# Loading x two tiles per transfer, and spreading the matmuls between the one-column groups, in a fused adaLN + sliding attention + SwiGLU kernel

## Chip, cores, metric

One Trainium2 chip, one core. The metric is device time in microseconds (us).

## The reference, cut to what matters

```python
mod = (silu(c) @ w_mod).reshape(1, 6, 1, -1)       # sa, ca, ga, sb, cb, gb
h = layernorm(x) * (1 + ca) + sa                   # x: 2048 x 1024, bf16
x = x + ga * attention(h, k_cache, v_cache, wq, wo)  # 32 q heads, 4 kv heads, last 512 keys
h = layernorm(x) * (1 + cb) + sb
x = x + gb * (silu(h @ w_gate) * (h @ w_up)) @ w_down
```

Only the beginning matters here: LayerNorm of the first 512 rows of x, the scale `1 + ca` and the shift `sa` (each a matrix-vector product with w_mod), and the first eight q heads.

## The kernel before

x is loaded as 128-row tiles of 256 KB, one transfer each. The loads shown all go through one queue, in this order; SyncE issues them.

```python
xt = [xpool.tile([P, D], BF16, ...) for tt in range(S // P)]
def load_x(tt):
    fetch(out=xt[tt], in_=x2d[tt * P:(tt + 1) * P, :])

for tt in range(QT):                 # QT = 4 tiles, the first 512 rows
    load_x(tt)
for half in range(DH):               # DH = 2
    load_wm(1, half)                 # scale part of w_mod, 1 MB
    load_wq8(2 * half)               # wq of the first 8 heads, 512 KB
    load_wq8(2 * half + 1)
load_wm(0, 0); ...; load_wm(0, 1)    # shift part of w_mod, 1 MB each
# [cut: k, v, further wq]
```

LayerNorm of the four tiles is spread over the engines: tile 0 has its statistics on VectorE, tile 1 on ScalarE (a sum, then squares), both are normalised on GpSimd; tiles 2 and 3 are done on VectorE. For all four tiles ScalarE turns the variance into the scaling factor (`rstd_0`, lines `mv` in the profile). TensorE transposes them in the order 0, 1, 2, 3.

```python
stats_0(0)                # VectorE
act_sum(1)                # ScalarE
nc.scalar.copy(out=siluc, in_=sil_ps)
rstd_0(0)                 # ScalarE, needs the statistics of tile 0
stats_0(2)                # VectorE
act_squares(1)            # ScalarE
warm(3); xpose_0(0, norm_0(0))                  # GpSimd, then TensorE
rstd_0(1, 1.0 / D); rstd_0(2); warm(5)
stats_0(3)
xpose_0(1, norm_0(1)); xpose_0(2, ln_norm(2))
rstd_0(3); n3 = ln_norm(3)
mod_cols(1, 0, ca1, True, (0,))                 # first use of the scale part of w_mod
xpose_0(3, n3)
# [cut: the scaled copies hs, then q matmuls for heads 0 to 6 on contraction tiles 0 to 5]
```

The q matmuls start before the shift `sa` is known: its contribution is added as a bias. `sa_mm` computes columns of `sa` with one-column matmuls, `sa_out` copies them (two small VectorE instructions), `sh_mm` multiplies them with wq, again one column each. `q0(g, (6, 7))` are the two last 512-column matmuls of head g, put between these groups:

```python
q0(0, (6, 7)); q0(1, (6, 7))
sa_mm(0, (0, 1))
q0(2, (6, 7))
sa_mm(0, (2, 3))
sa_out(0)
q0(3, (6, 7))
sh_mm(0, range(5))                  # needs sa_out(0)
q0(4, (6, 7))
sh_mm(0, (5, 6))
# [cut: ln_mod]
sa_mm(1, (0,))
q0(5, (6, 7))
sa_mm(1, (1, 2, 3))
sa_out(1)
q0(H0 - 1, (6,)); q0(H0 - 1, (7,))  # H0 = 7
sh_mm(1, range(H0))                 # needs sa_out(1)
```

Of the kernel before, what the change touches and what calls it, by code (L numbers as in the profile page):

```python
# [11 lines left out]
BF16 = mybir.dt.bfloat16  # L12
# [576 lines left out]
def fast_path(ctx, tc, flag, A_x, A_k_cache, A_v_cache, A_wq, A_wo, B_x, B_w_gate, B_w_up,  # L589
# [4 lines left out]
    P = 128  # L594
    _, S, D = A_x.shape
    _, Hkv, Sk, Dh = A_k_cache.shape
    HD = A_wq.shape[1]
    H = HD // Dh
# [6 lines left out]
    QT = TCW // P  # L605
# [11 lines left out]
    x2d = A_x.flatten_outer_dims()  # L617
# [12 lines left out]
    xpool = ctx.enter_context(tc.tile_pool(name="xres", bufs=1))  # L630
# [21 lines left out]
    def big(name, shape=(P, 2, 512), dt=FP32):  # L652
        return psp.tile(list(shape), dt, name=name, tag="s", bufs=2)
# [6 lines left out]
    def pin(ins, what="steps"):  # L660
        return tc.keep_in_program_order(ins) if stage[what] else ins

    def fetch(out, in_):
        pin(nc.sync.dma_start(out=out, in_=in_), "dma")
# [19 lines left out]

    c_r = const.tile([DT, P], BF16, name="c_r")
    nc.scalar.dma_start(out=c_r, in_=c_v)
    xt = [xpool.tile([P, D], BF16, name=f"x{tt}", tag=f"x{tt}") for tt in range(S // P)]

    def load_x(tt):
        fetch(out=xt[tt], in_=x2d[tt * P:(tt + 1) * P, :])  # L690

    wm_tiles = {}

# [13 lines left out]
    H0 = 7  # L707
# [4 lines left out]
        load(t, wq_v[:, 2 * i:2 * i + 2, 0:8 * P])  # L712
        wq8.append(t)

    for tt in range(QT):
        load_x(tt)
    for half in range(DH):
        load_wm(1, half)
        load_wq8(2 * half)
# [115 lines left out]
    def at(k, f, *a):  # L835
        tasks.setdefault(k, []).append((f, a))
# [200 lines left out]
    def w0(g, dt):  # L1037
        return wq8[dt // 2][:, dt % 2, g * P:(g + 1) * P]

    def q0(g, dts, src=None):  # L1040
        for dt in dts:
            nc.tensor.matmul(q0_ps[g], lhsT=w0(g, dt),  # L1042
                             rhs=hs[dt // 4][:, dt % 4, :] if src is None else src[:, dt, :],
                             start=(dt == 0), stop=(dt == DT - 1 and g != H0 - 1))
# [4 lines left out]
    def sh_mm(half, heads):  # L1049
        for g in heads:  # L1050
            for i in range(4):
                dt = 4 * half + i
                nc.tensor.matmul(one_ps[:, 1 + half, g:g + 1], lhsT=w0(g, dt),  # L1053
                                 rhs=sa_bf[:, dt:dt + 1], start=(i == 0), stop=(i == 3))

    def sa_mm(half, tiles):
        for i in tiles:
            c = 4 * half + i
            for dt in range(DT):
                nc.tensor.matmul(one_ps[:, 0, c:c + 1],  # L1060
                                 lhsT=wm_tiles[(0, half)][:, dt, i * P:(i + 1) * P],
                                 rhs=siluc[:, dt:dt + 1], start=(dt == 0), stop=(dt == DT - 1))

    def sa_out(half):
        c = slice(4 * half, 4 * half + 4)
        nc.vector.tensor_copy(out=sa[:, c], in_=one_ps[:, 0, c])
        nc.vector.tensor_copy(out=sa_bf[:, c], in_=sa[:, c])
# [4 lines left out]
    for i in range(2):  # L1072
        t = big("q_ps")
# [10 lines left out]
    q0(0, (6, 7))  # L1084
    q0(1, (6, 7))
    sa_mm(0, (0, 1))
    q0(2, (6, 7))
    sa_mm(0, (2, 3))
    sa_out(0)
    q0(3, (6, 7))  # L1090
    sh_mm(0, range(5))
    q0(4, (6, 7))
# [1 line left out]
    for dt in range(4):  # L1094
        ln_mod(("h1", 0), dt, ca1, sa)
    sa_mm(1, (0,))
    q0(5, (6, 7))
    sa_mm(1, (1, 2, 3))
    sa_out(1)
    q0(H0 - 1, (6,))  # L1100
    q0(H0 - 1, (7,))
    sh_mm(1, range(H0))

    for i in range(2):
# [188 lines left out]
    for vec, dst, starts in ((2, gcol[0], (1, 9)), (4, cb1, (17, 25)), (3, sb, (33, 41)),  # L1293
# [8 lines left out]
        elif vec in (2, 5):  # L1302
            at(k, store_gate, vec // 5)
            at(k + 3, load_gate, vec // 5, gb_bc if vec == 5 else ga_bc)
    for tt in range(QT, S // P):
        cc, t = divmod(tt, QT)
        at(max((cc - 1) * H - 16, 0) + 2 + 2 * t, load_x, tt)
    for hg in range(H // 4):
        for i in range(2):
            for j in range(2):  # L1310
# [132 lines left out]
def kernel(tc, *args):  # L1443
    nc = tc.nc
    with tc.tile_pool(name="guard", bufs=1) as gp:
        flag = gp.tile([1, 1], I32, name="flag")
        over = fast_path(tc, flag, *args)
        with tc.If(over > 0):
            general_path(tc, *args)
# [30 lines left out]
```

## Time and profile before

| | before |
|---|---|
| time, median of 3 runs | 1272.11 us (1271.86 to 1272.19) |
| span of the profiled run | 1270.0 us |
| first q matmul starts | 11.43 us |
| first score matmul starts | 29.91 us |

From the profile page of the kernel before: the span, the busy time of each engine, and the chain of work that ended last.

```profile
span 1270.0 us, 18162 instructions
...
PE 1262.5 (99%) x7589; PEld 641.1 (50%) x7589; DVE 609.4 (48%) x1332; ACT 335.1 (26%) x440; POOL 4.2 (0%) x15
...
PE 99%; ACT 0%; DMA 0%; POOL 0%; issue 0%; DVE 0%; SPq 0%
```

TensorE (PE) is the limit nearly throughout. So the change can only act where PE still waits: in about the first 30 us. What is won or lost there should shift all the rest, and in the traces it does: in the nine later profiles that record every matmul, the shift against the kernel before is the same at 31 us and at the last matmul, to 0.01 us.

The timeline of TensorE before (start in us, duration in us, engine, line, operation, output<-inputs, shape, count; in brackets how long the engine was idle before it, and what ended that). L960 are the transposes, L785 and L1060 one-column products with w_mod, L1042 q matmuls, L1053 the bias columns, L1210 the first score matmuls.

```profile
9.08 1.07 PE L960 MATMUL h_ps<-ident,xn 128*128 128x128 bf16 x16 [0.23 <-POOL xn L989]
10.08 0.35 PE L785 MATMUL mod_ps<-siluc,wm 128*128 128x1 bf16 x8
...
11.43 4.58 PE L1042 MATMUL q_ps<-hs,wq 128*128 128x512 bf16 x20
15.85 0.94 PE L785 MATMUL mod_ps<-siluc,wm 128*128 128x1 bf16 x32
...
22.26 0.54 PE L1060 MATMUL one_ps<-siluc,wm 128*128 128x1 bf16 x16
...
23.50 0.59 PE L1042 MATMUL q_ps<-hs,wq 128*128 128x512 bf16 x2
24.09 0.64 PE L1053 MATMUL one_ps<-sa_bf,wq 128*128 128x1 bf16 x20
...
26.46 0.59 PE L1042 MATMUL q_ps<-hs,wq 128*128 128x512 bf16 x2
27.05 0.84 PE L1053 MATMUL one_ps<-sa_bf,wq 128*128 128x1 bf16 x28
...
29.91 1.03 PE L1210 MATMUL s_ps<-qT,kT 128*128 128x512 bf16 x4
```

How to read it: the durations of neighbouring matmuls overlap (the page gives a mean of 379 ns for one 512-column q matmul, while they start 0.216 us apart), so the distance between starts is what counts. Twenty-six q matmuls (from 16.65 us, not shown) fill the time up to 22.26 us, 0.216 us each; sixteen one-column matmuls, with their weight loads, fill 23.09 to 23.50 us (not shown), 25.6 ns each. Two q matmuls start at 23.50, so PE could go on at 23.93, but the bias columns start at 24.09: a gap of 0.16 us. The same gap stands between 26.46 + 0.43 = 26.89 and 27.05 us.

The timeline of VectorE before: statistics of tiles 0 and 2, then the normalisation of tiles 2 and 3 (one line for both).

```profile
3.49 1.29 DVE L845 BATCH_NORM_STATS2 st<-x 128x6 f32<-128x512 bf16 x2 [1.95 <-DMA x<-in_A_x_dram]
...
5.72 1.29 DVE L845 BATCH_NORM_STATS2 st<-x 128x6 f32<-128x512 bf16 x2 [0.69 <-DMA x<-in_A_x_dram]
...
8.64 1.29 DVE L864 TENSOR_SCALAR xn<-x,mv 128x1024 bf16<-128x1024 bf16 x2
```

The trace also records each of the 16 completions of a transfer; a wait ends with the last of them. In the kernel before, the x tiles were complete at 3.47, 4.09, 5.69 and 7.17 us, the first half of the scale part of w_mod at 10.03 us, the two halves of the shift part at 22.05 and 25.13 us.

### The profile page before, as it was taken

The numbers are of one execution on the slowest core, as the hardware profiler recorded it, in microseconds if no ns is written. First come the engines' busy times: TensorE is split into PE (matmuls) and PEld (weight loads), VectorE is DVE, ScalarE is ACT, GpSimd is POOL, SyncE is SP. The second block draws the span as 40 slices with busy tenths as digits, with TensorE's granted clock in tenths as the row PEclk, the third lists the DMA queues.
The fourth block names the chain that finished last, engine by engine and source line by source line (L and its number), as shares of the span: only waits on it lengthen the run. The fifth ranks groups of instructions, "written<-read, shape, count | busy, mean of one in ns | idle before, by whom it ended". The sixth has DMA issues, their size and how long they took to land.

```text
span 1270.0 us, 18162 instructions
## 1 busy us (share of the span) xinstructions
PE 1262.5 (99%) x7589; PEld 641.1 (50%) x7589; DVE 609.4 (48%) x1332; ACT 335.1 (26%) x440; POOL 4.2 (0%) x15
## 2 busy tenths in 40 slices
PE   9999999999999999999999999999999999999998
PEld 4555555555555555555554444444444444444444
DVE  5665658785678664677564631311222112221122
ACT  3543334343333433334341111011100111011100
POOL 1000000000000000000000000000000000000000
PEclk9999999999999999999999999999999999999999
DMA  9897657879456655454575479336633565425702
GB/s 290 209 252 180 166 141 168 173 165 219 121 136 175 150 138 153 113 154 113 121 206 143 136 227 247 95 95 212 211 114 105 169 213 181 158 91 168 246 15 71
DMA packets 306891, 204.46 MB, mean 161 GB/s; under 512 B 145649, under 2 KB 303345, under 8 KB 306802
## 3 DMA queue, kind: packets, MB, share of 16 engines
q1 hardware_dynamic: 301890, 199.03, 58.3%
q10 hardware_dynamic: 4912, 4.20, 1.0%
q8 instruction: 61, 1.00, 0.3%
q14 instruction: 28, 0.23, 0.1%
HBM read 165.94 MB, written 4.21 MB: 134 GB/s over the span
## 4 chain that ended last, share of the span: by engine, by line
PE 99%; ACT 0%; DMA 0%; POOL 0%; issue 0%; DVE 0%; SPq 0%
PE gu_ps L1356 30%; PE a_ps L1274 17%; PE q_ps L1199 16%; PE d_ps L1376 15%; PE o_ps L1242 9%; PE s_ps L1210 9%; PE q_ps L1042 1%; DMA x<-in_A_x_dram 0%; PE one_ps L1053 0%; PE mod_ps L785 0%; PE one_ps L1060 0%; PE h_ps L960 0%; ACT junk L981 0%; POOL xn L989 0%; ACT junk L975 0%
## 5 line engine op out<-in xcount | busy, mean ns | idle before, releaser
L1212 ACT ACTIVATE pT<-s_ps 128x1024 bf16<-128x1024 f32 x256 | 249.4, 1020 | 347.4 <-PE s_ps L1210 347.4
L1274 PE MATMUL a_ps<-wo,oT 128*128 128x512 bf16 x1024 | 241.9, 379 | 0.0
L1199 PE MATMUL q_ps<-hT,wq 128*128 128x512 bf16 x960 | 227.1, 379 | 0.0
L1362 DVE TENSOR_TENSOR guT<-gu_ps,sg 128x512 bf16<-128x512 f32 x112 | 77.5, 692 | 286.8 <-ACT sg L1361 286.7
L1356 PE MATMUL gu_ps<-hT,wg 128*128 128x512 bf16 x896 | 211.7, 379 | 0.0
L1361 ACT ACTIVATE sg<-gu_ps 128x512 bf16<-128x512 f32 x112 | 66.9, 597 | 488.7 <-PE gu_ps L1356 480.1
L1376 PE MATMUL d_ps<-wd,guT 128*128 128x512 bf16 (+2 forms) x952 | 194.2, 366 | 0.0
L1356 PE MATMUL gu_ps<-hT,wu 128*128 128x512 bf16 x672 | 163.3, 379 | 0.0
L1274 PEld LDWEIGHTS <-oT 128*128 128x128 bf16 x1024 | 100.2, 98 | 120.6
L946 DVE CAST qT<-q_ps 128x512 bf16<-128x512 f32 x121 | 83.6, 691 | 154.8 <-PE q_ps L1199 154.5
L1199 PEld LDWEIGHTS <-wq 128*128 128x128 bf16 x960 | 93.9, 98 | 113.3
L1376 PEld LDWEIGHTS <-guT 128*128 128x128 bf16 x952 | 90.9, 98 | 102.9
L1242 PEld LDWEIGHTS <-pT 128*128 128x128 bf16 x2048 | 126.6, 98 | 30.2
L1356 PEld LDWEIGHTS <-wg 128*128 128x128 bf16 x896 | 87.6, 98 | 105.5
L1242 PE MATMUL o_ps<-v_sb,pT 128*128 128x129 bf16 x2048 | 137.0, 220 | 0.0
L1210 PE MATMUL s_ps<-qT,kT 128*128 128x512 bf16 x512 | 131.5, 379 | 0.0
L1356 PEld LDWEIGHTS <-wu 128*128 128x128 bf16 x672 | 65.8, 98 | 79.3
L1229 DVE TENSOR_TENSOR oq<-o_ps,rl 128x256 bf16<-128x256 f32 (+2 forms) x256 | 100.6, 419 | 3.9
L1380 DVE TENSOR_TENSOR f<-d_ps,gb_bc 128x512 f32<-128x512 f32 (+2 forms) x34 | 22.4, 660 | 140.8 <-PE d_ps L1376 140.8
L1210 PEld LDWEIGHTS <-kT 128*128 128x128 bf16 x512 | 44.9, 98 | 30.9 <-issue 0.5
L1282 DVE TENSOR_TENSOR acc<-a_ps,acc 128x512 f32<-128x512 f32 x64 | 44.0, 688 | 32.6 <-PE a_ps L1274 32.6
L1356 PE MATMUL gu_ps<-hT,v_sb 128*128 128x512 bf16 x224 | 57.5, 379 | 0.0
(101 smaller groups left out, 426.7 us busy)
## 6 DMA issues: line engine op xcount, KB each, us to landing
wq<-in_A_wq_dram SPq DMA_DIRECT2D x64, 512.0 KB
wo<-in_A_wo_dram SPq DMA_DIRECT2D x64, 512.0 KB
wg<-in_B_w_gate_dram SPq DMA_DIRECT2D x56, 512.0 KB
wd<-in_B_w_down_dram SPq DMA_DIRECT2D x56, 512.0 KB
wu<-in_B_w_up_dram SPq DMA_DIRECT2D x42, 512.0 KB
v_sb<-in_B_w_up_dram SPq DMA_DIRECT2D x14, 512.0 KB
x<-in_A_x_dram SPq DMA_DIRECT2D x16, 256.0 KB
wm<-in_w_mod_dram SPq DMA_DIRECT2D x4, 1024.0 KB
```

The source lines that it names most:

```text
L946: nc.vector.tensor_copy(out=t, in_=q_ps)
L1199: nc.tensor.matmul(q_ps, lhsT=w, rhs=hT[("h1", cc)][:, dt, :], start=(dt == 0), stop=(dt == DT - 1))
L1210: nc.tensor.matmul(s_ps[:, i, :], lhsT=kT[:, kv, j * P:(j + 1) * P], rhs=qT[g], start=True, stop=True)
L1212: nc.scalar.activation(out=p[:, 2 * jj:2 * jj + 2, :], in_=s_ps, func=ACT.Exp, scale=scale)
L1229: nc.vector.tensor_tensor(out=dst, in0=ps[:, s0:s0 + cnt, 0:Dh], in1=sc, op=ALU.mult)
L1242: nc.tensor.matmul(o_slot["ps"][:, s_, :], lhsT=pT[g][:, j, t * P:(t + 1) * P], rhs=v_sb[:, kv, j, 0:VN], start=(j == 0), stop=(j == WT - 1))
L1274: nc.tensor.matmul(a_ps, lhsT=oT[(cc, 2 * q + i)][:, hh % 4, t * P:(t + 1) * P], rhs=wo_tiles[(cc, q, dh, i)][:, hh % 4, :], start=(hh == ...
L1282: nc.vector.tensor_tensor(out=acc[(cc, t)][:, dsl], in0=a_ps, in1=acc[(cc, t)][:, dsl], op=ALU.add)
L1356: nc.tensor.matmul(ps[:, n, :], lhsT=gu_w[(cc, fg, nm, dt // 4)][:, dt % 4, fi * P:(fi + 1) * P], rhs=hT[("h2", cc)][:, dt, :], start=(dt ...
L1361: nc.scalar.activation(out=g, in_=ps[:, 0, :], func=ACT.Silu)
L1362: nc.vector.tensor_tensor(out=guT[(cc, fg)][:, fi, :], in0=ps[:, 1, :], in1=g, op=ALU.mult)
L1376: nc.tensor.matmul(d_ps, lhsT=guT[(cc, f // 4)][:, f % 4, t * P:(t + 1) * P], rhs=wd_tiles[(cc, dh, f // 4)][:, f % 4, c0:c0 + w], start=( ...
```

## The change

Intent: fewer, larger transfers for x, and one 512-column matmul at a time rather than a pair between the one-column groups, with one more q matmul behind each pair of copies of `sa`.

```diff
-    xt = [xpool.tile([P, D], BF16, name=f"x{tt}", tag=f"x{tt}") for tt in range(S // P)]
-    def load_x(tt):
-        fetch(out=xt[tt], in_=x2d[tt * P:(tt + 1) * P, :])
+    x2t = [xpool.tile([P, 2, D], BF16, name=f"x{i}", tag=f"x{i}") for i in range(S // P // 2)]
+    xt = [x2t[tt // 2][:, tt % 2, :] for tt in range(S // P)]
+    def load_x2(i):
+        fetch(out=x2t[i], in_=x2d[2 * i * P:2 * (i + 1) * P, :].rearrange("(t p) d -> p t d", p=P))
...
-    for tt in range(QT):
-        load_x(tt)
+    for i in range(QT // 2):
+        load_x2(i)
...
-    q0(2, (6, 7))
+    q0(2, (6,))
     sa_mm(0, (2, 3))
     sa_out(0)
+    q0(2, (7,))
     q0(3, (6, 7))
...
-    q0(5, (6, 7))
+    q0(5, (6,))
     sa_mm(1, (1, 2, 3))
     sa_out(1)
-    q0(H0 - 1, (6,))
-    q0(H0 - 1, (7,))
+    q0(5, (7,))
+    q0(H0 - 1, (6, 7))
     sh_mm(1, range(H0))
...
-    for tt in range(QT, S // P):
+    for tt in range(QT, S // P, 2):
         cc, t = divmod(tt, QT)
-        at(max((cc - 1) * H - 16, 0) + 2 + 2 * t, load_x, tt)
+        at(max((cc - 1) * H - 16, 0) + 2 + 2 * t, load_x2, tt // 2)
```

## The prediction

> **What bounds the kernel now.** TensorE. The page gives PE 99% busy at full clock; the chain of waits is 99% PE. A 512-column matmul starts every 0.216 us (26 in 16.65-22.26, timeline). The view of waits names no PE stall after the head, so only about the first 30 us can gain or lose, and that should reach the end one to one.
>
> The head, from the timeline and the landing events:
> - The x tiles land near 3.5, 4.1, 5.7 and 7.15 us; the first w_mod half at 10.0, the first wq piece at 11.36, the last w_mod half at 25.1. From 2.5 to 25 us the queue always has work (250 to 370 GB/s in the windows): bandwidth limits it, not issue.
> - LayerNorm statistics take VectorE 1.29 us per tile plus 0.21 and start at 3.49, 5.72, 7.19. Normalised tile 3 is ready near 9.9, its transposes start at 10.29, the first q matmul at 11.43, just after its wq.
> - From there PE has about 0.1 us of gaps up to 15.85, and two of 0.16 us, at 23.93 and 26.89, where bias columns wait for two VectorE copies of the shift vector (0.16 + 0.17 us).
>
> **What the change does.**
> 1. It moves one q matmul behind each pair of copies. 0.216 us covers 0.16 us: up to 0.32 us gained on the critical path, no work added. One-column matmuls keep their pitch of 25.6 ns (16 in 0.41 us)[...].
> 2. Two transfers of 512 KB replace four of 256 KB. Issues take about 0.46 us each, so weights are issued 0.9 us earlier, but queue behind the same bytes. [...] tile 0 now waits for tile 1, tile 2 for tile 3. Statistics of tile 0 start near 4.1, of tile 2 near 6.5 to 7.1.
> 3. From tile 2 on VectorE works serially: two statistics and two normalisations, about 4.2 us, then transposes and scaling, 1.1 us. So the first q matmul starts about 5.3 us after the second landing (an estimate from these durations): 11.8 to 12.4, 0.4 to 1.0 us later. About 0.1 us is absorbed.
> 4. Later x tiles: nothing.
>
> **Sum.** +0.4 to +1.0, -0.3, -0.1: about +0.3 us. **Predicted 1272.4 us, range 1271.2 to 1273.8.** Chances: faster by over 2% 0.01, within 2% 0.98, slower by over 2% 0.01.
>
> **What would show it.** Timeline: no PE gap before the two bias groups. Statistics of tile 0 at 4.0 or later, of tile 2 at 6.5 or later; ScalarE and GpSimd reach tile 0 about 0.4 us later; first q matmul at 11.8 to 12.4; w_mod landings within 0.3 us of before. From 40 us the same pattern, shifted equally.
>
> **What would make it wrong.** Some 2 KB x packets between 3.4 and 6.3 us take 350 to 950 ns, against about 80 later. If transfer boundaries cause that, tiles 2 and 3 may land near 5.5: nothing is late and the time falls by 0.3 to 0.8 us. If the second transfer lands after 7.3, the loss passes 1 us. VectorE may also become the limit between first scaling and the copies of the transposed tile.

The trace of the kernel before shows the DMA engines busy throughout (a share of 0.95 to 1.16 in windows of 2 to 3 us from 2 to 25 us); that bandwidth and not issue sets the landings was the author's reading of this and is not shown.

## More of the kernel before

The chain of waits before, in order of time (start, duration, what). This is the head of what led to the first transposes of tile 1.

```profile
1.19 2.90 DMA x<-in_A_x_dram
...
4.11 1.15 ACT junk L975 x2
...
5.87 1.25 ACT junk L981 x2
...
7.83 1.20 POOL xn L989
```

Tile 1 of x lands at 4.09 us; ScalarE sums it (4.11) and squares it (5.87); GpSimd normalises it (7.83); PE transposes it at 9.08 us.

## The result, and the profile after

The changed kernel took 1272.28 us (median of 6 runs, 1272.17 to 1272.67); the kernel before took 1272.09 us on the same chip (median of 6, 1271.86 to 1272.59). A ratio in this document is the mean time of one kernel's runs over the mean of the other's runs of the same rounds, so it is not quite the ratio of the medians. Here it is 1.0002, with a 95% interval of 0.9989 to 1.0015: the same.

From the page of the changed kernel:

```profile
span 1270.4 us, 18154 instructions
...
PE 1262.5 (99%) x7589; PEld 641.2 (50%) x7589; DVE 609.4 (48%) x1332; ACT 335.0 (26%) x440; POOL 4.2 (0%) x15
...
PE 99%; DMA 0%; ACT 0%; DVE 0%; POOL 0%; issue 0%; POOLq 0%
```

The timeline of TensorE after, the lines that answer to those above (line numbers have moved by one or two):

```profile
9.94 1.07 PE L961 MATMUL h_ps<-ident,xn 128*128 128x128 bf16 x16 [0.24 <-POOL xn L990]
10.85 0.34 PE L786 MATMUL mod_ps<-siluc,wm 128*128 128x1 bf16 x8
...
12.10 4.59 PE L1043 MATMUL q_ps<-hs,wq 128*128 128x512 bf16 x20
16.53 0.94 PE L786 MATMUL mod_ps<-siluc,wm 128*128 128x1 bf16 x32
...
22.94 0.54 PE L1061 MATMUL one_ps<-siluc,wm 128*128 128x1 bf16 x16
...
23.96 0.81 PE L1043 MATMUL q_ps<-hs,wq 128*128 128x512 bf16 x3
24.60 0.64 PE L1054 MATMUL one_ps<-sa_bf,wq 128*128 128x1 bf16 x20
...
26.75 0.81 PE L1043 MATMUL q_ps<-hs,wq 128*128 128x512 bf16 x3
27.40 0.84 PE L1054 MATMUL one_ps<-sa_bf,wq 128*128 128x1 bf16 x28
...
30.26 1.03 PE L1212 MATMUL s_ps<-qT,kT 128*128 128x512 bf16 x4
```

Three things are to be seen. The first q matmul starts at 12.10 us, 0.67 us late. The two gaps are gone: three q matmuls start at 23.96 and the bias columns follow at 24.60, which is 3 x 0.216 us later; the same at 26.75 and 27.40 us. The first score matmul starts at 30.26 us, so of 0.67 us lost, 0.32 us are won back and 0.35 us remain. This shift stays to the end: a group of output-projection matmuls starts at 300.17 us before and at 300.52 us after, and the last store is issued at 1266.07 us before and at 1266.42 us after. Loading the later x tiles in pairs did nothing that shows.

The chain of waits after:

```profile
0.73 3.74 DMA x<-in_A_x_dram
...
4.50 1.30 DVE st L846 x2
...
6.07 0.30 ACT mv L966
...
6.72 1.25 ACT junk L982 x2
...
8.69 1.20 POOL xn L990
```

Tiles 0 and 1 are both complete at 4.48 us, as one transfer. ScalarE must wait for the statistics of tile 0, which VectorE starts only now (4.50), and so begins the squares of tile 1 at 6.72 us rather than 5.87. GpSimd follows at 8.69 rather than 7.83, and PE transposes tile 1 at 9.94 rather than 9.08 us.

The timeline of VectorE after:

```profile
4.50 1.28 DVE L846 BATCH_NORM_STATS2 st<-x 128x6 f32<-128x512 bf16 x2 [2.96 <-DMA x<-in_A_x_dram]
...
5.95 1.23 DVE L846 BATCH_NORM_STATS2 st<-x 128x6 f32<-128x512 bf16 x2
...
8.97 1.64 DVE L865 TENSOR_SCALAR xn<-x,mv 128x1024 bf16<-128x1024 bf16 x2 [0.16 <-ACT mv L967]
```

The statistics of tile 2 do not wait for x at all: the second pair was complete at 5.83 us, while VectorE was still busy with tile 0. The prediction had put this landing at 6.5 to 7.1 us and had taken it for the one that decides. Why the first pair lands at 4.48 us, when the same bytes in two transfers were there at 4.09 us, is not shown.

The w_mod halves were complete at 8.81 us (scale, 10.03 before) and at 21.39 and 24.49 us (shift, 22.05 and 25.13 before). They are earlier by 0.6 to 1.2 us, but PE uses the shift halves only from 22.94 and 25.74 us on and gains nothing from it.

### The profile page after: what moved, and what is told of

It reads as the page before. It is cut to its first block, busy times and chain, and to the rows that moved or that the text cites. A ratio compares the mean times of both kernels' runs of the same rounds, so it can differ in the third digit from the quotient of the medians.

```text
span 1270.4 us, 18154 instructions
## 1 busy us (share of the span) xinstructions
PE 1262.5 (99%) x7589; PEld 641.2 (50%) x7589; DVE 609.4 (48%) x1332; ACT 335.0 (26%) x440; POOL 4.2 (0%) x15
## 4 chain that ended last, share of the span: by engine, by line
PE 99%; DMA 0%; ACT 0%; DVE 0%; POOL 0%; issue 0%; POOLq 0%
PE gu_ps L1358 30%; PE a_ps L1276 17%; PE q_ps L1201 16%; PE d_ps L1378 15%; PE o_ps L1244 9%; PE s_ps L1212 9%; PE q_ps L1043 1%; DMA x<-in_A_x_dram 0%; PE one_ps L1061 0%; PE mod_ps L786 0%; PE h_ps L961 0%; PE one_ps L1054 0%; DVE st L846 0%; ACT junk L982 0%; POOL xn L990 0%; ACT mv L966 0%
```

## The experiments

Kernels are compared only within the same rounds. The theory after the result: the first q matmul is late because tiles 0 and 1 now land together and late, through ScalarE and GpSimd. Rival: the second pair, through VectorE, as predicted. Second question: does the order of the matmuls gain its 0.32 us by itself? One further idea, all four tiles in one transfer, did not build (a deadlock when scheduled) and is left open.

| kernel | mean, us | before, us | difference | first q, us | first score, us |
|---|---|---|---|---|---|
| e0 changed, again | 1272.24 | 1272.33 | -0.09 | 12.05 | 30.21 |
| e1 order only | 1271.84 | 1272.33 | -0.49 | 11.33 | 30.17 |
| e2 merged loads only | 1272.67 | 1272.33 | +0.34 | 12.17 | 30.66 |
| e3 tiles 0, 1 single | 1273.41 | 1272.33 | +1.08 | 11.61 | 30.10 |
| e4 tiles 2, 3 single | 1272.60 | 1272.13 | +0.47 | 12.05 | 30.23 |
| e6 whole pairs moved | 1272.09 | 1272.13 | -0.04 | 11.28 | 30.26 |
| e7 tiles 2, 3 by ScalarE | 1273.68 | 1272.13 | +1.55 | 12.25 | 30.40 |
| e3b = e3 again | 1273.46 | 1272.13 | +1.33 | 12.59 | 30.77 |
| e8 shift columns late | 1273.83 | 1271.99 | +1.84 | 11.57 | 32.06 |
| e1b = e1 again | 1272.05 | 1271.99 | +0.06 | 11.81 | 29.95 |
| e9 changed, third time | 1272.55 | 1271.99 | +0.56 | 12.12 | 30.28 |
| e10 one more ahead | 1272.63 | 1272.11 | +0.52 | 11.83 | 31.74 |

The starts are of each kernel's one profiled run. The runs of before scatter from 1271.66 to 1273.00 us, so differences under about 0.3 us in this table say little alone. By the stricter measure, the 95% intervals of the ratios (each about 0.0013, or 1.7 us, to either side), only the slowdown of e7 is clear of zero, and the interval of e8 begins at it. There is a second source of scatter: from the start of the last matmul to the end of the span the profiles show 4.79 to 5.32 us, and that has nothing to do with the head. So the causes below rest on the traces.

### e0: the changed kernel again

No edit.

> The changed kernel again, beside the others on the same chip. Expected as before: +0.2 to +0.4 us against the kernel before; first q matmul at 12.1 us, the score matmuls start about 0.35 us late.

Measured: -0.09 us against before, five times from 1272.12 to 1272.45. The size missed (before was slower); the trace agrees: first q matmul at 12.05, first score matmul 0.30 us late against the profiled run of before.

### e1 and e1b: the order alone

```diff
 # x in four single transfers, as in the kernel before
-    q0(2, (6, 7))
+    q0(2, (6,))
     sa_mm(0, (2, 3))
     sa_out(0)
+    q0(2, (7,))
 # and the same for head 5
```

> Only the moved q matmuls, x loaded in four transfers as before. Theory (the order gains, the load loses): about -0.32 us against before, the two PE gaps of 0.16 us gone, first q matmul at 11.43 as before, the first score matmul at about 29.6 instead of 29.91. Rival (splitting pairs costs PE time in the head): 0 or slower.

> The order alone again, for the size of its gain on this chip: 0.2 to 0.5 us under before if the first result holds; scatter of some tenths, since the w_mod halves land about when they are needed.

Measured: -0.49 us in the first, +0.06 us in the second, where the expected gain of 0.2 to 0.5 us did not come. Both gaps are gone in both traces. But the first score matmul started at 30.17 us, not at 29.6, because PE had to wait for the shift part of w_mod. The timeline of TensorE of e1:

```profile
22.62 0.55 PE L1060 MATMUL one_ps<-siluc,wm 128*128 128x1 bf16 x16 [0.28 <-DMA wm<-in_w_mod_dram]
...
25.64 0.35 PE L1060 MATMUL one_ps<-siluc,wm 128*128 128x1 bf16 x8
```

PE was ready for the first shift columns at 22.18 us (16.57 us plus 26 x 0.216 us) and began at 22.62; the eight columns at 25.64 could have begun at 25.43. The w_mod halves landed at 22.57 and 25.59 us. So in this run the order won 0.32 us and lost 0.65 us to late weights. In the trace of e1b there was no such wait, but there tile 2 of x landed late, at 6.52 us, and the first w_mod half of the scale too, at 10.41 us; by the intervals given below either puts the first q matmul at 11.81 us, where it was. The expectation of 29.6 us for the first score matmul was not met in either run; the vanished gaps were. That splitting pairs costs PE time, as the rival had it, is not seen.

### e2: the merged loads alone

```diff
 # load_x2 as in the changed kernel; the q matmuls in the old order
```

> Only the merged x loads, q matmuls in their old order. Theory: about +0.67 us against before, first q matmul at 12.1, both gaps of 0.16 us still there. Rival (the order change made the loss): 0.

Measured: +0.34 us, times from 1272.51 to 1272.87. First q matmul at 12.17 us; the bias columns still wait (two q matmuls start at 24.25, so PE is free at 24.68, and the columns start at 24.85). In the trace the load makes the loss; the order does not. There the first score matmul is 0.75 us later than in the profiled run of before, but the times differ by 0.34 only. The profiled run of before was one of its quick ones (1271.82 us; that of e2 took 1272.56, which is 0.74 us more and agrees with the traces): it waited nowhere for the shift halves, which other runs with single loads did (0.65 us in e1, 0.79 us in e6).

### e3 and e3b: tiles 0 and 1 single, tiles 2 and 3 in one transfer

```diff
-    for i in range(QT // 2):
-        load_x2(i)
+    for tt in range(2):
+        fetch(out=xt[tt], in_=x2d[tt * P:(tt + 1) * P, :])
+    load_x2(1)
```

> The changed kernel, but tiles 0 and 1 of x loaded singly, tiles 2 and 3 in one transfer. My theory now (the loss comes from the landing of tiles 0 and 1, through ScalarE and GpSimd): transposes of tile 1 at about 9.1 as before, first q matmul at 11.25 to 11.5, time -0.3 to -0.5 us against before. The theory of the prediction (the second transfer decides, through VectorE): first q matmul 0.3 us or more after 11.43, time 0 or slower against before.

> The same kernel as e3 again, because its five times scattered over 3.3 us and the profile did not show why. If the scatter belongs to this kernel: again up to 1275 us and a mean near 1273. If it was chance: 1271.8 to 1272.3.

Measured: +1.08 and +1.33 us. For e3 a gain had been expected; a miss. The timeline of VectorE of e3:

```profile
3.46 1.29 DVE L847 BATCH_NORM_STATS2 st<-x 128x6 f32<-128x512 bf16 x2 [1.91 <-DMA x<-in_A_x_dram]
...
6.37 1.29 DVE L847 BATCH_NORM_STATS2 st<-x 128x6 f32<-128x512 bf16 x2 [1.38 <-DMA x<-in_A_x_dram]
```

Tile 0 starts early again (3.46), and the transposes of tile 1 at 9.07 us as expected. But now the second pair landed at 6.34 us (7.32 in e3b), VectorE waited for it, and the first q matmul started 5.27 us after this landing, at 11.61 us (12.59 in e3b). That is the chain of the prediction, with its 5.3 us. The 11.61 us of e3 lies between what the two theories had asked for (11.25 to 11.5, and 11.73 or later). So neither theory is the whole: whichever chain ends last decides.

The scatter was repeated: 1272.14 to 1275.46 and 1272.05 to 1276.38 us. The slowest run of each had a mean granted clock of 0.998 and 0.997; all runs of the kernel before had 0.999 or 1.000. These two runs were not profiled. The drop of the clock that e8 and e10 show below is the likely cause, but here it is not shown; and one such drop costs 1.7 us there, while these two runs took 2.2 and 2.9 us more than the next slowest of the same kernel.

### e4: tiles 0 and 1 in one transfer, tiles 2 and 3 single

```diff
-    for i in range(QT // 2):
-        load_x2(i)
+    load_x2(0)
+    for tt in range(2, QT):
+        fetch(out=xt[tt], in_=x2d[tt * P:(tt + 1) * P, :])
```

> The changed kernel, but tiles 2 and 3 of x loaded singly, tiles 0 and 1 in one transfer. If the landing of the first pair decides, through ScalarE and GpSimd: first pair lands near 4.5, transposes of tile 1 near 9.9, first q matmul at 11.9 to 12.2, time as the changed kernel (0 to +0.3 us against before). If the second pair decides, through VectorE: first q matmul near 11.4, time -0.3 or less. Slow packets (over 250 ns) between 4 and 10 us: some 20 or more if the number of transfers makes them, under 8 if single loads of tiles 0 and 1 do.

Measured: +0.47 us, above the 0 to +0.3 expected. The profiled run took 0.78 us more than that of before (1272.60 against 1271.82); 0.33 us of it stand at the first score matmul, and 0.46 us come only after the last matmul. The first pair landed at 4.43, tile 2 at 5.05 and tile 3 at 5.92 us, and the first q matmul started at 12.05 us, as in the changed kernel. The timeline of TensorE of e4:

```profile
9.89 1.07 PE L962 MATMUL h_ps<-ident,xn 128*128 128x128 bf16 x16 [0.24 <-POOL xn L991]
10.80 0.34 PE L787 MATMUL mod_ps<-siluc,wm 128*128 128x1 bf16 x8
```

Early tiles 2 and 3 did not help: the first pair decides. It is a close test, since the first w_mod half landed late here, at 10.63 us, and would have allowed 12.03 us. But PE began the scale columns at 10.80 us, 0.17 us after this landing and straight after the transposes of tiles 1 and 2, which had waited for GpSimd. There were 14 slow packets, between the two numbers that I had set.

### e6: pairs kept whole

```diff
-    q0(2, (6, 7))
     sa_mm(0, (2, 3))
     sa_out(0)
+    q0(2, (6, 7))
     q0(3, (6, 7))
 # and the same for head 5
```

> x as before; the pairs of q matmuls kept whole, but the pair of head 2 and that of head 5 moved behind the copies of the shift vector. If a matmul behind the copies is what gains: as the run with the order alone, about -0.3 to -0.5 us, both gaps gone. If splitting the pairs gains something by itself: less than half of that.

Measured: -0.04 us, scattered from 1271.62 to 1272.53; a gain of 0.3 to 0.5 us had been expected. In the trace both gaps are gone, exactly as with the split pairs, so it is the further matmul behind the copies that closes them. The profiled run waited 0.62 and 0.17 us for the two shift halves, which landed at 22.70 and 25.68 us. By the time alone the run cannot say whether splitting also gains something. The traces say that it does not: from the first q matmul to the first score matmul, less the waits for the shift halves, it is 18.19 us here (18.98 - 0.79) and 18.19 us in e1 with its split pairs (18.84 - 0.65).

### e7: four single transfers, two of them issued by ScalarE

```diff
-    for i in range(QT // 2):
-        load_x2(i)
+    for tt in range(2):
+        fetch(out=xt[tt], in_=x2d[tt * P:(tt + 1) * P, :])
+    for tt in range(2, QT):
+        nc.scalar.dma_start(out=xt[tt], in_=x2d[tt * P:(tt + 1) * P, :])
```

> The changed kernel, but x tiles 0 to 3 in four single transfers, tiles 2 and 3 issued by ScalarE, so that SyncE issues the weights as early as in the changed kernel. If the earlier issue brings the weights sooner: the first w_mod half lands at 8.8 to 9.5, few slow packets. If the number of transfers decides: near 10, 20 slow packets or more between 4 and 10 us. First q matmul at 11.2 to 11.5 either way, unless ScalarE is late by its two issues[...].

Measured: +1.55 us; two of five runs had a granted clock of 0.998 and took 1274.67 and 1276.08 us. The first w_mod half landed early, at 8.68 us, with 3 slow packets on the main queue, although x came in four transfers. But tile 3, by then alone on the other queue, landed only at 8.38 us, 3.38 us after tile 2 and hardly before the 1 MB of the w_mod half. VectorE waited for it until 8.40 us, and the first q matmul started at 12.25 us. The expectation for the weights held, the one for the first q matmul did not.

### e8: shift columns late

```diff
+    for g in range(5):
+        q0(g, (6, 7))
+    sa_mm(0, range(4))
+    sa_out(0)
+    q0(5, (6,))
+    sh_mm(0, range(H0))
+    q0(5, (7,)); q0(H0 - 1, (6,))
+    sa_mm(1, range(4))
+    sa_out(1)
+    q0(H0 - 1, (7,))
+    sh_mm(1, range(H0))
 # in place of the interleaved order; x in four single transfers
```

> x in four single transfers as before; the q matmuls that need no w_mod are put ahead of the shift-vector columns, and one q matmul stays behind each pair of copies. If the single-load kernels lose their time to late w_mod halves (needed at 22.2 and 25.4 us, landed at 22.0 to 22.7 and 25.1 to 25.7 in the profiles): first q matmul at 11.3 to 11.45, no PE wait before the first shift columns, at most 0.25 us before the second, first score matmul at 29.5 to 29.8, time 0.4 to 0.7 us under before and under the changed kernel by as much. If the waits did not matter: as the run with the order alone.

Measured: +1.84 us; a miss, with two causes. The timeline of TensorE, and the windows (stretch, length, busy us and instruction count of PE, PEld, DVE, ACT and POOL, then the granted clock, DMA share and GB/s):

```profile
25.09 0.84 PE L1053 MATMUL one_ps<-sa_bf,wq 128*128 128x1 bf16 x28 [0.46 <-DVE sa_bf L1067]
...
27.61 0.84 PE L1053 MATMUL one_ps<-sa_bf,wq 128*128 128x1 bf16 x28 [0.46 <-DVE sa_bf L1067]
...
28.75 3.52 PE L1042 MATMUL q_ps<-hT,wq 128*128 128x512 bf16 x8
32.06 1.12 PE L1205 MATMUL s_ps<-qT,kT 128*128 128x512 bf16 x4
```

```profile
24.00:26.00 2.00, 1.54 (x55) 1.38 (x53) 1.30 (x6) 0.00 (x0) 0.00 (x0) 1.00 1.64 272
26.00:28.00 2.00, 1.54 (x50) 1.38 (x50) 1.09 (x5) 0.55 (x1) 0.00 (x0) 1.00 0.78 195
28.00:30.00 2.00, 2.00 (x25) 0.98 (x22) 1.68 (x4) 2.00 (x4) 0.00 (x0) 0.71 1.98 219
30.00:32.00 2.00, 2.00 (x6) 0.69 (x5) 2.00 (x4) 0.12 (x1) 0.00 (x0) 0.50 0.79 148
```

The wait for w_mod was gone, as meant. But with a single q matmul behind each pair of copies PE waited for them, 0.36 us each time (24.73 to 25.09 by the pitch; the profile says 0.46 after the last recorded matmul). The kernel before had two matmuls there and waited 0.16 us; the change has three and waits for nothing. And the clock of TensorE fell to half at about 28.84 us for about 3.4 us (from the windows: 0.71 of full over 28 to 30 us means half from 28.84 on; with 0.50 over 30 to 32 and 0.94 over 32 to 34 us, 1.70 us of full clock are lost, which at half is 3.4 us), so that eight q matmuls that should take 1.73 us took 3.3 us. Four of the five runs had a clock of 0.997 or 0.998.

### e9: the changed kernel a third time

No edit.

> The changed kernel a third time, as the partner of the two others on the same chip: within 0.3 us of before, its five times within 0.5 us of each other, because no w_mod half is late in it.

Measured: +0.56 us, a miss (within 0.3 us of before had been expected, and a scatter within 0.5); four times from 1272.20 to 1272.38 and one of 1273.57, at a clock of 1.000. That one run is not explained. The trace is that of the changed kernel: first pair at 4.49, first q matmul at 12.12, first score matmul at 30.28 us.

### e10: the order, and one more q matmul ahead

```diff
     q0(0, (6, 7)); q0(1, (6, 7))
+    q0(2, (6,))
     sa_mm(0, (0, 1))
-    q0(2, (6,))
+    q0(2, (7,))
     sa_mm(0, (2, 3))
     sa_out(0)
-    q0(2, (7,))
-    q0(3, (6, 7))
+    q0(3, (6, 7)); q0(4, (6,))
     sh_mm(0, range(5))
-    q0(4, (6, 7))
+    q0(4, (7,))
 # shown against the order of the change; x in four single transfers
```

> x in four single transfers as before; the order of the change, and one more q matmul moved ahead of the first shift-vector columns (so the first w_mod half of the shift is needed 0.216 us later, still three q matmuls behind each pair of copies). If late w_mod halves cost the order-only kernel some of its gain: the wait before the first shift columns is at most 0.25 us, time 0.2 to 0.6 us under before, the mean granted clock 0.999 or more in all runs (the order with one matmul behind each copy lowered it). If waits for w_mod do not matter, or x lands late by chance: within 0.2 us of before.

Measured: +0.52 us, a miss in time and in clock; the five runs fall into two groups: 1273.74 and 1273.31 us at a clock of 0.998, and 1272.11, 1272.09 and 1271.90 us at 1.000. The windows of the profiled run, which is of the first group:

```profile
24.00:26.00 2.00, 1.92 (x45) 1.40 (x44) 1.62 (x6) 0.00 (x0) 0.00 (x0) 1.00 1.86 270
26.00:28.00 2.00, 1.92 (x56) 1.63 (x56) 0.97 (x4) 1.02 (x2) 0.00 (x0) 0.99 0.66 165
28.00:30.00 2.00, 2.00 (x8) 0.62 (x5) 1.90 (x4) 1.65 (x3) 0.00 (x0) 0.50 1.87 186
30.00:32.00 2.00, 2.00 (x8) 0.80 (x7) 1.73 (x4) 0.00 (x0) 0.00 (x0) 0.66 0.93 192
```

PE waited 0.05 us at most for the shift halves, as meant. But the clock fell to half at about 27.95 us for about 3.4 us (0.99, 0.50 and 0.66 of full over the last three windows, 1.70 us lost), and the first score matmul started at 31.74 us, 19.91 us after the first q matmul rather than 18.16. No better version came of this. The order-only kernel had the lower mean beside the changed kernel (by 0.40 and 0.49 us; by the medians 0.34 and 0.38); against the kernel before its gain is not settled.

## Why the prediction was right, point by point

The size was right: predicted 1272.4, measured 1272.28 us; predicted +0.3 us, in the traces +0.35 us. The times alone do not show it: by the medians it was +0.19 us here, by the means -0.09 us in e0 and +0.56 us in e9. The reason was half right, and that the first q matmul fell into the predicted 11.8 to 12.4 us was luck: a landing put too late and a chain left out made up for each other.

**The covered gaps: right.** Predicted 0.32 us. From the first q matmul to the first score matmul it is 18.48 us before and 18.16 us after; 18.49 us in e2 (old order) and 18.14 to 18.18 us in e0, e9, e1b, e3b and e4 (new order, no wait for weights).

**"So the first q matmul starts about 5.3 us after the second landing": this is the step that failed.** The chain is real and its length was right, but it was not the last one: the second pair landed at 5.83 us and by this chain would have allowed 11.11 us. The first pair, through ScalarE and GpSimd, set 12.10 us. The first q matmul starts at the latest of three times, which the runs give to within 0.02 us:

- first pair: 7.15 us after tile 1 lands, where tile 0 came first (e6: 4.14 to 11.28; e1: 4.18 to 11.33), but 7.62 us after the landing, where both come in one transfer (after: 4.48 to 12.10; e0: 4.43 to 12.05; e2: 4.55 to 12.17; e4: 4.43 to 12.05; e9: 4.49 to 12.12). The 0.47 us more come from the statistics of tile 0, for which ScalarE then waits;
- second pair: 5.28 us after tile 2 lands (e3: 6.34 to 11.61; e3b: 7.32 to 12.59; e1b, 6.52 to 11.81, fits this line and the next one alike);
- scale part of w_mod: 1.40 us after its first half lands (before: 10.03 to 11.43; e8: 10.16 to 11.57; e10: 10.43 to 11.83).

In the profiled run of before the w_mod half decided, with 11.24 us for the first pair close behind. After the change the first pair decides. The predicted 0.4 to 1.0 us held 0.67 us, which is made up of another sum: +0.39 us for the later landing of tile 1 (4.09 to 4.48), +0.47 us for tile 0 landing with it, -0.19 us because the w_mod half no longer decides. e7 does not fit the second line, since there tile 3 came 3.4 us after tile 2, and the first q matmul 3.87 us after tile 3.

**"Statistics of tile 0 start near 4.1, of tile 2 near 6.5 to 7.1": wrong in size.** 4.50 and 5.95 us. I had let both landings be those of the later tile in the old kernel. That the wait ends with the last of the 16 completions is what the trace shows: the sixteen of the first pair came from 3.79 to 4.48 us, and the statistics started at 4.50.

**"w_mod landings within 0.3 us of before": wrong.** The first half came 1.22 us earlier, and 0.46 to 1.20 us earlier in e0, e2 and e9. The prediction had named slow packets as a way to be wrong. Packets on the main queue of over 250 ns that start between 4 and 10 us: 12 to 34 in the six profiles with four x transfers on it, 14 to 21 in the three with three, 1 to 4 in the four with two, and 3 in e7, with two on each of two queues. So two x transfers on a queue go with few slow packets, three or four with many; why is not shown. That they make the half late is not shown either: it landed at 9.42 us in e1, with 31 of them, and at 9.57 us in e0, with 1. It is also issued 0.86 us earlier in the changed kernel (1.74 us, 2.60 before).

**"About 0.1 us is absorbed": not seen.** From the first q matmul to the second group of scale columns it is 4.42 us before and 4.43 us after.

**Later x tiles: right.** The shift of 0.35 us is the same at 300 us and at the end.

**What the prediction missed.** Before, the shift halves of w_mod land just when PE needs them (22.05 and 25.13 us, used at 22.26 and 25.22). This may be why single loads scatter: e1 and e6 waited 0.65 and 0.79 us there. The four profiles with two pairs show no such wait. Part of what the merged load loses at the start it gets back in the runs where the single loads wait; this would explain why merging costs 0.75 us between two traces, but 0.34 us (e2 against before), 0.40 us (e0 against e1) and 0.49 us (e9 against e1b) in mean times. That the waits in runs without a profile make the difference is inferred, not shown.

## What to carry to other kernels

Before merging transfers at the start of a kernel, write down every chain that leads from a landing to the first useful work, with its length, and take the latest: the merged transfer here delayed the chain of its first tile (tile 0 was complete at 4.48 us rather than 3.47), and the tile of which you think first need not be on the last chain. Where a dependent group waits for a short copy, count the time of the whole hand-over (here 0.59 us before, 23.50 to 24.09, of which the two copies are 0.33) and put so much independent work behind it. And look at the granted clock after any reordering: in the profiles of e8 and e10 it fell to half for about 3.4 us, which cost 1.7 us.

## What the traces show besides, and leave open

- The clock. In the profiled runs of e8 and e10 it stood at half for about 3.4 us (1.70 us of full clock lost in the windows of each). PE was not idle before: its records show it busy 77% of 24 to 28 us in e8 and 96% in e10, but most of its matmuls there had one column. Such rows alone do not do it: e6 has two rows of 32 of them, and its five runs show 0.999 or 1.000. A mean clock of 0.997 or 0.998 was seen in four of five runs of e8 and two of five of e10, and in no run of the kernel before or of the changed one (0.999 or more in each run listed). One run each of e3 and e3b and two of e7, which have the matmul order of the changed kernel, show 0.997 or 0.998 as well. What makes the clock fall, what keeps it up, and why only some runs of a kernel drop is not shown.
- An instruction fetch. The traces have a fetch of 16 KB that takes about 1.05 us, at 15.7 us before and at 16.3 us after. In the changed kernel the sixteen completions of the transfers that land from 10.15 to 17.22 us lie 0.4 us apart, and 1.7 us at the next transfer (fifteen by 20.19 us, the last at 21.39). That the fetch causes this is possible, not shown: in the kernel before, the sixteen lie 1.6 us apart already at 10.03 us.
